# Four two-bank PSUM tiles in place of a four-bank work tile and two fixed pairs, in a delta-rule and mixture-of-experts kernel

## The chip, the core and the metric

The kernel runs on one core of a Trainium2 chip. A core has a matrix engine (TensorE, PE in the profile), three engines for elementwise work (VectorE or DVE, ScalarE or ACT, GpSimd or POOL) and one that issues DMA transfers (SyncE, SP). PSUM is the memory that matrix products go to: eight banks of 512 fp32 numbers in each of 128 partitions in this kernel's use of it. The metric is the device time of the core in microseconds; the figure quoted is the median of several runs.

## The reference

Two computations follow each other. The first is a linear-attention recurrence with a delta rule, for 4 batch entries, 8 heads, 768 tokens and a head dimension of 48:

```
k_n = k / (norm(k) + 1e-6)
for t in range(768):
    y[t]  = q[t] @ state
    v_old = k_n[t] @ state
    state = state + beta[t] * outer(k_n[t], v[t] - v_old)
```

Its output, with the 8 heads side by side, is x (768 tokens of width 384 for each batch entry). The second computation has four attention experts with head dimension 64; two of them are taken for each token:

```
logits = x @ w_gate;  top 2 of 4;  w = softmax over those two
for each expert e:
    q, k, v = x @ wq[e], x @ wk[e], x @ wv[e]
    a  = causal softmax(q k^T / 8)
    ye = a @ v @ wo[e]
    out += w[e] * ye      (where e is among the token's two)
```

Everything is fp32. The kernel computes all four experts for every token and gives the unused ones the weight zero.

## The kernel before, in words

**Blocks.** The work is cut into six units: unit n is batch half n//3 (two batch entries) and token block n%3 (256 tokens). The recurrence is worked in chunks of 64 tokens, c = 0 to 3 in a unit, with 2 batch entries x 8 heads laid over partitions and columns, so that one step of the program is 16 to 64 small matrix products. Within a chunk the recurrence becomes a triangular system, solved once per unit, and the state passes from chunk to chunk.

**The order.** The program has no loop over this work. Each step is a small function, and the string `ORDER` lists steps by name with their arguments, for example `gk.1.0:01` (step gk, unit 1, chunk 0, PSUM banks 0 and 1). The last lines of the kernel walk through the string and call one function after the other under a manual schedule, so this order is the order of the instructions on every engine and in SP's queue. An engine does its instructions one after the other; what one engine needs of another is waited for with semaphores, which the framework puts in from the reads and writes of tiles. A step that writes PSUM carries its place in the string, and a later step that reads it carries the same place.

**PSUM.** Before the change there are three tiles: `PO` (name po in the profile, two banks) for the attention product av and for the dummy products of `fill`; `PA` (pa, two banks) for the state chain; `PR` (pr, four banks) for all else, with `two(k)` giving a pair of banks (any two of the four, "02" is banks 0 and 2) and `one(k)` a single bank.

**The steps**, with the engine that does them. All matrix products go through the helper `mm`, line 175, so PE's instructions have that line in the profile, but for the transposes (L667 and L748).

- Loads, issued by SP: lk (keys and queries of a chunk, two DMAs, 192 KB), lh (one half of it, keys or queries; defined, and not used before), lv (values), lc, ld, lz (constants), lw (weights, split into two fp32r parts by wh on ACT and wl on POOL).
- Preparing a unit: gk (k times k within a chunk) and its readers ek (ACT), or for unit 0 en (DVE) and ed (ACT and DVE); gq (k times q) and its reader eq (DVE). si, so and sn are 32x32 transposes by DVE over a whole unit (L342, L424, L420). pre (DVE) makes the norms. The solve is 15 steps sb on DVE for unit 0 and 32 steps sv on POOL for each other unit (L385, L387).
- Completing the solve: for unit 0 the products zp with their readers ze (ACT or DVE, by i) and preparations zx (the DVE one for chunks is L438); for the others sc1 (ACT), ma, its reader ea (ACT), mc (POOL, L479), mb, its reader eb (ACT).
- The state chain of each chunk: ks, ex (DVE, L507), uu, eu (ACT, L516), st, es (DVE, L530), all on `PA`; vt (POOL, L498) scales the values. The chunk's output: yq, yu into a pair of `PR`, read by eh (ACT, L554) and el (DVE, L558), which split it into two fp32r parts. hx are six small DMAs per half unit that move rows of it to other partitions.
- Projections: pj into one bank, read by ph (ACT, L584) and pl (DVE, L587); pv into two, read by ev (ACT, L600) and eg (DVE, L603); gates (DVE) makes the routing weights.
- Attention: mx (scores for the row maximum) and its reader em (DVE, L651); mp, mr, er (L671) bring the maximum to the layout of the scores; sc (scores) and its reader xp (ACT, exp, L705); av, with the readers oa (ACT, L731) and ob (DVE, L735); nm (DVE, L739 to L742) scales.
- Output: ft (transposes, L748) into one bank, read by fh (ACT, L751) and fl (DVE, L754); fo (times wo) for each 128 tokens into one bank, read by eo (ACT, L765); do (SP, L769) stores 128 tokens.
- `fill` runs a number of dummy products (tile zb) that nothing reads.

Buffers: eight for a chunk's keys and queries, three for its values, two for a unit's system (`TG`, `BB`), three for exp scores (`AT`), two output tiles `OT`.

Of the kernel before, what the change touches and what calls it, by code (L numbers as in the profile page):

```python
# [46 lines left out]
sb.1 en.2:01 sb.2 sb.3 sb.4 sb.5 sv.1.1 sv.1.2 sb.6 sv.1.3 sb.7 sv.1.4 sb.8 sb.9 sv.1.5 sb.10 sv.1.6 sb.11 sb.12
sv.1.7 sb.13 sb.14 sv.1.8 sb.15 sv.1.9 so.0 sv.1.10 sv.1.11 zx.0.0 sn.0 fill.8 zp.0.1:2 sv.1.12 zp.0.0:3 ze.0.0:3
sv.1.13 ze.0.1:2 sv.1.14 zx.1.0 fill.8 zp.0.2:0 zx.0.1 zp.0.3:1 sv.1.15 ze.0.2:0 zp.1.0:3 zp.1.1:2 ze.0.3:1 ze.1.0:3
sv.1.16 ze.1.1:2 fill.2 zp.0.4:0 sv.1.17 zx.1.1 ze.0.4:0 zp.1.2:1 ze.1.2:1 zp.1.3:3 zx.2.2 uu.0.0 ze.1.3:3 gk.2.0:02  # L50
eu.0.0 zp.1.4:1 ek.2.0:02 st.0.0 lv.0.3 zx.2.3 es.0.0 zp.2.1:3 ze.1.4:1 ks.0.1 ze.2.1:3 yu.0.0:02 ex.0.1 gq.0.3:13
eh.0.0:02 eq.0.3:13 sv.1.18 el.0.0:02 fill.6 zp.3.0:1 sv.1.19 zp.3.1:3 ze.3.0:1 zp.2.3:0 ze.3.1:3 zp.2.0:2 vt.0.3
ze.2.3:0 zp.3.3:1 ze.2.0:2 zp.3.2:3 sv.1.20 ze.3.3:1 gq.0.2:02 lw.2 ze.3.2:3 zp.2.2:1 sv.1.21 eq.0.2:02 zp.3.4:3
sv.1.22 ze.2.2:1 lv.0.2 ze.3.4:3 gq.0.1:02 eq.0.1:02 zp.2.4:1 sv.1.23 ze.2.4:1 yq.0.1:03 vo uu.0.1 sv.1.24 lk.2.1 wh.2
eu.0.1 sv.1.25 fill.7 st.0.1 vt.0.2 yu.0.1:03 lv.1.0 es.0.1 gq.1.0:12 eh.0.1:03 sv.1.26 ks.0.2 eq.1.0:12 sv.1.27
ex.0.2 fill.2 yq.0.2:12 sv.1.28 el.0.1:03 lk.2.2 uu.0.2 sv.1.29 eu.0.2 gk.2.1:03 hx.0.0 sv.1.30 sv.1.31 ek.2.1:03
yu.0.2:12 st.0.2 lv.1.1 es.0.2 eh.0.2:12 fill.4 gq.1.1:03 sv.1.32 ks.0.3 eq.1.1:03 ex.0.3 fill.2 yq.0.3:03 el.0.2:12
lk.2.3 uu.0.3 eu.0.3 gk.2.2:12 vt.1.0 sn.1 ek.2.2:12 st.0.3 vt.1.1 yu.0.3:03 lv.1.2 wl.2 eh.0.3:03 fill.4 gq.1.2:12
es.0.3 wl.4 eq.1.2:12 ks.1.0 el.0.3:03 gk.2.3:12 so.1 ek.2.3:12 pj.0.0.0:0 hx.0.1 vt.1.2 si.2 ma.1.0:3 sc1.1.1
pv.0.1:12 mc.1.0 ea.1.0:3 pre.2.0 pre.2.1 ph.0.0.0:0 pre.2.2 pj.0.0.1:3 ev.0.1:12 eg.0.1:12 pre.2.3 sc1.1.0 pre.2.4  # L60
pre.2.5 pj.0.1.0:1 pl.0.0.0:0 ph.0.0.1:3 ex.1.0 pl.0.0.1:3 mx.0.1.1.0.0:02 ph.0.1.0:1 sv.2.1 mb.1.0:3 sv.2.2
em.0.1.1.0.0:02 pl.0.1.0:1 sv.2.3 mx.0.0.0.0.0:02 sv.2.4 eb.1.0:3 ma.1.1:1 em.0.0.0.0.0:02 sv.2.5 mx.0.0.1.0.0:02
ea.1.1:1 mc.1.1 pj.0.1.1:3 em.0.0.1.0.0:02 sv.2.6 sv.2.7 mb.1.1:0 ph.0.1.1:3 sv.2.8 pl.0.1.1:3 mx.0.1.0.1.0:12
eb.1.1:0 sv.2.9 em.0.1.0.1.0:12 sv.2.10 fill.7 mx.0.1.0.0.0:13 mx.0.0.1.1.0:02 em.0.1.0.0.0:13 em.0.0.1.1.0:02 sv.2.11
mx.0.0.0.1.0:13 em.0.0.0.1.0:13 pv.0.0:02 sv.2.12 mp.0.0 sv.2.13 yq.1.0:13 ev.0.0:02 eg.0.0:02 gates.0.0 sv.2.14
uu.1.0 lk.3.0 mx.0.1.1.1.0:02 eu.1.0 sv.2.15 em.0.1.1.1.0:02 fill.3 st.1.0 gates.0.1 mr.0.0:0 lv.1.3 sv.2.16 yu.1.0:13
er.0.0:0 eh.1.0:13 es.1.0 fill.4 gk.3.0:02 sv.2.17 el.1.0:13 ks.1.1 ek.3.0:02 sv.2.18 ex.1.1 yq.1.1:13 gates.0.2
lk.3.1 uu.1.1 vt.1.3 gq.1.3:02 mp.0.1 eu.1.1 eq.1.3:02 st.1.1 sv.2.19 yu.1.1:13 lv.2.0 es.1.1 gq.2.0:02 eh.1.1:13
sv.2.20 ks.1.2 eq.2.0:02 ex.1.2 sv.2.21 fill.2 yq.1.2:02 el.1.1:13 lk.3.2 uu.1.2 sv.2.22 eu.1.2 gk.3.1:13 hx.1.0
ek.3.1:13 st.1.2 vt.2.0 yu.1.2:02 lv.2.1 es.1.2 sv.2.23 ks.1.3 eh.1.2:02 yq.1.3:13 ex.1.3 sv.2.24 lk.3.3 el.1.2:02  # L70
uu.1.3 sv.2.25 eu.1.3 gq.2.1:02 sv.2.26 eq.2.1:02 yu.1.3:13 st.1.3 sv.2.27 eh.1.3:13 gk.3.2:02 lv.2.2 es.1.3 sv.2.28
ek.3.2:02 el.1.3:13 vt.2.1 ks.2.0 ex.2.0 gk.3.3:13 hx.1.1 sv.2.29 sv.2.30 ek.3.3:13 pj.1.0.1:0 sv.2.31 si.3 pv.1.1:12
ph.1.0.1:0 sv.2.32 pl.1.0.1:0 pj.1.1.1:3 ev.1.1:12 pre.3.0 vt.2.2 sn.2 pj.1.1.0:0 ph.1.1.1:3 so.2 ph.1.1.0:0
pl.1.1.1:3 sc1.2.0 pl.1.1.0:0 fill.8 ma.2.1:3 eg.1.1:12 sc1.2.1 pre.3.1 ma.2.0:0 mc.2.1 pre.3.2 pre.3.3 pv.1.0:12
ea.2.1:3 mc.2.0 pre.3.4 pre.3.5 ea.2.0:0 mb.2.1:3 eg.1.0:12 gates.1.0 ev.1.0:12 mb.2.0:0 sv.3.1 gates.1.1 eb.2.1:3
sv.3.2 mr.0.1:1 gates.1.2 sv.3.3 pj.1.0.0:2 sv.3.4 eb.2.0:0 er.0.1:1 sv.3.5 sv.3.6 yq.2.0:13 ph.1.0.0:2 uu.2.0 sv.3.7
lk.4.0 pl.1.0.0:2 eu.2.0 sv.3.8 fill.4 mx.1.1.1.0.0:02 yu.2.0:13 em.1.1.1.0.0:02 sv.3.9 st.2.0 eh.2.0:13 lv.2.3 es.2.0
gq.2.3:02 sv.3.10 el.2.0:13 ks.2.1 sv.3.11 ex.2.1 yq.2.1:13 eq.2.3:02 lk.4.1 uu.2.1 sv.3.12 eu.2.1 mx.1.0.0.0.0:02
em.1.0.0.0.0:02 yu.2.1:13 sv.3.13 st.2.1 eh.2.1:13 gk.4.0:02 lv.3.0 es.2.1 vt.2.3 ek.4.0:02 el.2.1:13 ks.2.2 sv.3.14
ex.2.2 sc.0.1.0.0:13 hx.2.0 sv.3.15 mx.1.0.0.1.0:02 xp.0.1.0.0:13 em.1.0.0.1.0:02 sv.3.16 fill.4 gq.2.2:13 eq.2.2:13  # L80
vt.3.0 gk.4.1:02 ek.4.1:02 yq.2.2:13 sv.3.17 uu.2.2 lk.4.2 sv.3.18 eu.2.2 fill.4 mx.1.0.1.1.0:02 st.2.2
em.1.0.1.1.0:02 sv.3.19 yu.2.2:13 lv.3.1 eh.2.2:13 es.2.2 sv.3.20 fill.3 gk.4.2:02 el.2.2:13 ks.2.3 ek.4.2:02 sv.3.21
ex.2.3 yq.2.3:13 lk.4.3 uu.2.3 lv.3.2 sv.3.22 gq.3.1:02 eu.2.3 eq.3.1:02 yu.2.3:13 vt.3.1 sc.0.0.0.0:02 eh.2.3:13
sv.3.23 el.2.3:13 sv.3.24 xp.0.0.0.0:02 gk.4.3:13 hx.2.1 sv.3.25 ek.4.3:13 fill.3 av.0.0.0.0 vt.3.2 sc.0.1.1.0:02
sv.3.26 oa.0.0.0 si.4 sv.3.27 pv.2.1:13 xp.0.1.1.0:02 sv.3.28 sv.3.29 ob.0.0.0 sv.3.30 sv.3.31 pre.4.0 gq.3.0:02
ev.2.1:13 eg.2.1:13 pre.4.1 sc.0.0.1.0:13 lk.5.0 pre.4.2 pre.4.3 sv.3.32 pre.4.4 xp.0.0.1.0:13 pre.4.5 eq.3.0:02
fill.8 pj.2.0.0:1 so.3 pj.2.1.0:3 ph.2.0.0:1 sv.4.1 pl.2.0.0:1 sc1.3.1 sv.4.2 sv.4.3 sn.3 mx.2.1.1.0.0:02 sv.4.4
av.0.0.1.0 ph.2.1.0:3 sv.4.5 pj.2.0.1:1 oa.0.0.1 sc1.3.0 sv.4.6 pl.2.1.0:3 sv.4.7 em.2.1.1.0.0:02 ma.3.1:3 ph.2.0.1:1
sv.4.8 ob.0.0.1 pl.2.0.1:1 mx.2.0.0.1.0:02 sv.4.9 ea.3.1:3 av.0.1.0.0 em.2.0.0.1.0:02 pj.2.1.1:1 sv.4.10 oa.0.1.0
nm.0.0 sv.4.11 ob.0.1.0 mx.2.0.0.0.0:03 sv.4.12 ph.2.1.1:1 av.0.1.1.0 em.2.0.0.0.0:03 mb.3.1:2 oa.0.1.1 sv.4.13  # L90
pl.2.1.1:1 mx.2.0.1.1.1:03 eb.3.1:2 sv.4.14 ob.0.1.1 ma.3.0:1 em.2.0.1.1.1:03 sv.4.15 mx.2.0.0.0.1:03 ea.3.0:1
ft.0.0:2 em.2.0.0.0.1:03 sv.4.16 mb.3.0:0 fh.0.0:2 nm.0.1 sv.4.17 mx.1.0.1.0.0:13 fl.0.0:2 eb.3.0:0 em.1.0.1.0.0:13
sv.4.18 fill.3 fo.0.0.1:2 mp.1.0 sv.4.19 mx.1.1.1.1.0:01 eo.0.0.1:2 fo.0.0.0:3 em.1.1.1.1.0:01 do.0.0.1 sv.4.20
mr.1.0:2 eo.0.0.0:3 pv.2.0:01 er.1.0:2 sv.4.21 do.0.0.0 sv.4.22 sc.1.0.0.0:23 sv.4.23 ev.2.0:01 eg.2.0:01 gates.2.0
sv.4.24 sc.1.0.0.1:01 xp.1.0.0.0:23 gates.2.1 sv.4.25 gates.2.2 mx.2.1.1.1.1:23 xp.1.0.0.1:01 sv.4.26 av.1.0.0.0
em.2.1.1.1.1:23 sv.4.27 mx.2.1.1.1.0:01 mx.2.0.0.1.1:23 sv.4.28 em.2.1.1.1.0:01 av.1.0.0.1 sv.4.29 mc.3.0 oa.1.0.0
em.2.0.0.1.1:23 fill.3 mx.1.1.0.1.0:01 em.1.1.0.1.0:01 mx.2.1.0.1.1:23 sv.4.30 uu.3.0 sv.4.31 eu.3.0 em.2.1.0.1.1:23
fill.3 gk.5.0:01 st.3.0 ob.1.0.0 ek.5.0:01 yu.3.0:23 lv.3.3 es.3.0 sv.4.32 ks.3.1 eh.3.0:23 yq.3.1:01 ex.3.1 lk.5.1
el.3.0:23 uu.3.1 mc.3.1 so.4 eu.3.1 gq.3.3:23 st.3.1 vt.3.3 yu.3.1:01 lv.4.0 eh.3.1:01 eq.3.3:23 sc1.4.0 el.3.1:01
fill.8 gq.4.0:23 eq.4.0:23 mx.2.0.1.1.0:01 hx.3.0 sc1.4.1 em.2.0.1.1.0:01 fill.3 sc.1.0.1.1:23 vt.4.0 sn.4  # L100
sc.1.0.1.0:01 xp.1.0.1.1:23 xp.1.0.1.0:01 gk.5.1:23 es.3.1 ek.5.1:23 fill.4 mx.1.1.0.0.0:01 ks.3.2 em.1.1.0.0.0:01
# [759 lines left out]
```

## Time and profile before

| | |
|---|---|
| median of 3 runs | 821.58 us (816.61 to 832.48) |
| profiled execution | 828.15 us |
| its span, first to last instruction | 826.4 us |
| mean granted TensorE clock | 0.732 of full |
| busy: PE, DVE, POOL, ACT | 69%, 35%, 27%, 24% of the span |
| DMA traffic | 30.04 MB, mean 36 GB/s |

The profile is of one execution, so its durations add up to its own time, 828.15 us, not to the median. "Busy" counts the time in which an engine has an instruction running; PE's busy time holds the dummy products too. A wait row names the engine and tile that waited, the line and engine whose end released it, and then total time, count and longest. A stage in the stretch view is given by its start and end in us from the span's start. The fp32 products are recorded as two instructions each.

### The profile page before, as it was taken

The numbers are of one execution on the slowest core, as the hardware profiler recorded it, in microseconds if no ns is written. First come the engines' busy times: TensorE is split into PE (matmuls) and PEld (weight loads), VectorE is DVE, ScalarE is ACT, GpSimd is POOL, SyncE is SP. The second block draws the span as 40 slices with busy tenths as digits, with TensorE's granted clock in tenths as the row PEclk, the third lists the DMA queues.
The fourth block names the chain that finished last, engine by engine and source line by source line (L and its number), as shares of the span: only waits on it lengthen the run. The fifth ranks groups of instructions, "written<-read, shape, count | busy, mean of one in ns | idle before, by whom it ended". The sixth has DMA issues, their size and how long they took to land. (4 is left out here: it accounts for less than half of the span.)

```text
span 826.4 us, 26105 instructions
## 1 busy us (share of the span) xinstructions
PE 571.5 (69%) x11987; PEld 480.8 (58%) x11987; DVE 292.4 (35%) x627; ACT 194.4 (24%) x344; POOL 225.5 (27%) x385
## 2 busy tenths in 40 slices
...
GB/s 189 127 0 2 21 61 109 3 1 100 78 2 43 67 68 20 3 20 24 46 69 31 21 2 22 11 3 31 59 2 51 30 10 21 17 4 1 18 7 59
DMA packets 15277, 30.04 MB, mean 36 GB/s; under 512 B 2880, under 2 KB 9024, under 8 KB 15168
## 3 DMA queue, kind: packets, MB, share of 16 engines
...
## 5 line engine op out<-in xcount | busy, mean ns | idle before, releaser
L651 DVE TENSOR_REDUCE mx<-pr 128x2 f32<-128x1024 f32 (+3 forms) x48 | 45.7, 956 | 110.1 <-PE pr L175 80.9
L385 POOL TENSOR_TENSOR bl<-bl,tp 128x30 f32<-128x30 f32 (+9 forms) x150 | 77.9, 519 | 11.7
L387 POOL TENSOR_TENSOR tp<-bl 128x30 f32<-128x30 f32 (+9 forms) x150 | 73.8, 492 | 10.9
L175 PE MATMUL pr<-xh,wqkh 128*128 128x256 f32 x288 | 58.9, 355 | 21.3 <-DVE kl L587 5.2
L705 ACT ACTIVATE at<-pr 128x768 f32<-128x768 f32 (+1 forms) x48 | 43.2, 916 | 118.8 <-PE pr L175 108.9
L498 POOL TENSOR_TENSOR kv<-kv,nt 128x384 f32<-128x384 f32 x24 | 20.4, 848 | 181.0 <-DMA kv<-in_kv_dram 150.7
L175 PEld LDWEIGHTS pr<-xh,wqkh 128*128 128x128 f32 x288 | 50.9, 253 | 26.3 <-DVE kl L587 5.7
L175 PE MATMUL pr<-kq 48*64 48x64 f32 x1536 | 46.7, 277 | 28.1 <-ACT at L705 5.9
L175 PE MATMUL pr<-kh,qh 64*128 64x512 f32 (+3 forms) x128 | 35.7, 557 | 41.5 <-DVE kl L587 8.8
L175 PE MATMUL po<-vs,at 64*64 64x65 f32 x2528 | 60.5, 252 | 2.1 <-issue 1.0
L175 PEld LDWEIGHTS pr<-kq 48*64 48x64 f32 x1536 | 38.9, 182 | 38.3 <-ACT at L705 6.8
L175 PEld LDWEIGHTS po<-vs,at 64*64 64x64 f32 x2528 | 54.4, 164 | 8.9 <-issue 4.4
L175 PE MATMUL pr<-qh,kh 64*128 64x256 f32 x192 | 41.2, 425 | 20.8 <-DVE mx L651 8.1
L175 PEld LDWEIGHTS pr<-kh,qh 64*128 64x128 f32 x128 | 16.4, 253 | 54.5 <-DVE ql L587 8.4
L175 PE MATMUL po<-zb 128*128 128x252 bf16 x211 | 44.3, 362 | 1.6 <-DVE zb L178 1.1
L479 POOL MEMSET tt<- 32x512 f32 x20 | 10.4, 518 | 109.8 <-PE pr L175 109.0
L175 PEld LDWEIGHTS pr<-qh,kh 64*128 64x128 f32 x192 | 23.0, 236 | 27.2 <-DVE mx L651 9.8
L175 PE MATMUL pr<-wvgh,xh 128*128 128x260 f32 x144 | 33.6, 373 | 3.3 <-DVE mx L651 2.0
L175 PE MATMUL pr<-qh,kl 64*128 64x256 f32 x192 | 32.0, 330 | 0.0
L175 PE MATMUL pr<-kq,sb 48*48 48x64 f32 x704 | 19.4, 267 | 18.2 <-ACT tt L320 5.2
L175 PE MATMUL pr<-ql,kh 64*128 64x256 f32 x192 | 31.9, 328 | 0.0
L175 PEld LDWEIGHTS pr<-wvgh,xh 128*128 128x128 f32 x144 | 28.7, 272 | 5.2 <-DVE mx L651 2.5
...
## 6 DMA issues: line engine op xcount, KB each, us to landing
kq<-in_kq_dram SPq DMA_DIRECT2D x48, 192.0 KB, 4.0
...
out_dram<-ot SPq DMA_DIRECT2D x24, 192.0 KB, 2.0
...
```

Of the source, the lines that this page charges most:

```text
L175: T.matmul(o, lhsT=a, rhs=b, start=start, stop=stop, skip_group_check=True)
L385: e.tensor_tensor(X[:, a:b, i + 1:], X[:, a:b, i + 1:], tv, op=OP.add)
L387: e.tensor_tensor(tv, R[:, :, i + 1:].to_broadcast([128, w, m]), X[:, a:b, i:i + 1].to_broadcast([128, w, m]), op=OP.mult)
L479: G.memset(TG[n % 2][r + 32:r + 64, MW * q:MW * q + MW, 0:32], 0.0)
L498: G.tensor_tensor(v, v, nt[n % 2][:, c * NP:c * NP + NP, None].to_broadcast([128, NP, HD]), op=OP.mult)
L651: V.tensor_reduce(d, two(k)[:, :, 0:w], axis=AX.X, op=OP.max)
L705: S.activation(at_of(n, b, y, kp)[:, :, 0:w], two(k)[:, :, 0:w], AF.Exp, scale=0.125)
```

## The change

PSUM becomes four tiles `ps0` to `ps3` of two banks each, `PP` in the code. The place in a step's name is now one digit, the tile: `two(k)` is the whole tile, `one(k)` its first bank. The tiles po and pa go; the state chain (ks, ex, uu, eu, st, es) and the attention product (av, oa, ob) take a tile by name, a new one for each step or chain link. `fill` takes a count and a tile and writes its second bank.

Steps that used one bank and come in pairs take the two banks of one tile: pj for queries and keys of a half unit (`isk` 0 and 1), zp by the parity of i, fo for the two halves of 256 tokens. ma and mb run over all 32 systems of a unit at once, into both banks; sc1, ea, mc and eb now go by halves of the partitions and no longer by halves of the systems, and of ea and eb one half is on ACT and the other on DVE. eo copies both halves of an output at once, from one tile of two banks into one `OT` of twice the size, and do stores 256 tokens with one DMA, so that there are 12 eo and 12 do in place of 24. lh is cut into two DMAs by partitions and is used for unit 0, keys and queries separately; the steps lk go from 24 to 20 and lh from 0 to 8.

The order is a new one. The matmuls of `fill` in it go from 210 to 85, and the one in `init` is removed. The number of steps goes from 1427 to 1368; each unit, chunk and head is still computed with the same products.

```diff
-init lk.1.0 lk.0.3 lz lc.0 lk.1.1 lk.0.0 lk.0.2 lk.0.1 lw.0 lk.1.2 lk.1.3 lc.1 lw.1 ld lv.0.1 lw.3 lv.0.0 lc.2 fill.8
-gk.1.0:01 ek.1.0:01 fill.7 gk.0.3:23 en.3:23 ed.3:23 fill.3 gk.1.1:01 ek.1.1:01 fill.4 gk.0.0:23 en.0:23 ed.0:23
-fill.4 gk.0.2:01 ed.2:01 fill.4 gk.0.1:23 wh.0 en.1:23 ed.1:23 wl.0 si.0 fill.8 gk.1.2:23 lw.6 ek.1.2:23 pre.0.0 wh.1
...
-fo.5.0.1:3 oa.5.1.1 ob.5.1.1 nm.5.1 fo.5.0.0:0 eo.5.0.1:3 do.5.0.1 eo.5.0.0:0 ft.5.1:2 do.5.0.0 fh.5.1:2 fl.5.1:2
-fill.8 fo.5.1.1:1 fo.5.1.0:3 eo.5.1.1:1 do.5.1.1 eo.5.1.0:3 do.5.1.0
+init lz lc.0 lh.0.1.0 lh.0.0.0 lh.0.2.0 lc.1 lh.0.3.0 fill.8:0 gk.0.1:0 lw.0 lc.2 ed.1:0 fill.2:1 gk.0.0:1 ld lk.1.1
+ed.0:1 fill.2:2 gk.0.2:2 lh.0.1.1 ed.2:2 lh.0.3.1 fill.6:3 gk.0.3:3 en.2:2 lh.0.2.1 ed.3:3 wh.0 lv.0.0 cb si.0 wl.0
+lk.1.3 cc lk.1.0 lk.1.2 pre.0.0 zm gk.1.1:2 lw.5 pre.0.1 ek.1.1:2 lv.0.1 zt lh.0.0.1 en.1:0 lw.1 lw.3 pre.0.2 lw.4
+lw.6 pre.0.3 pre.0.4 pre.0.5 vt.0.0 gk.1.3:2 en.0:1 ek.1.3:2 sb.1 sb.2 fill.8:0 gk.1.0:0 sb.3 sb.4 ek.1.0:0 sb.5
+fill.8:1 gk.1.2:1 sb.6 sb.7 ek.1.2:1 sb.8 sb.9 wh.5 sb.10 vt.0.1 si.1 fill.8:2 gq.0.0:2 wl.5 lk.2.0 wh.1 pre.1.0 wl.1
+wh.3 pre.1.1 wh.4 wl.3 pre.1.2 wh.6 wl.4 pre.1.3 wl.6 sb.11 sb.12 sb.13 pre.1.4 sb.14 pre.1.5 sb.15 so.0 sv.1.1 sv.1.2
...
+oa.5.1.1:0 ob.5.1.1:0 nm.5.1 fo.5.0.1:2 eo.5.0:2 ft.5.1:3 do.5.0 fh.5.1:3 fl.5.1:3 fill.8:1 fo.5.1.0:1 fo.5.1.1:1
+eo.5.1:1 do.5.1
...
-    PO = ps.tile([128, 2, 512], F32, name="po")
-    PA = ps.tile([128, 2, 512], F32, name="pa")
-    PR = ps.tile([128, 4, 512], F32, name="pr")
+    PP = [ps.tile([128, 2, 512], F32, name=f"ps{i}") for i in range(4)]
 
     def two(k):
-        a, b = (int(x) for x in k)
-        return PR[:, a:b + 1:b - a]
+        return PP[int(k)]
 
     def one(k):
-        return PR[:, int(k)]
-
-    def fill(k=1):
-        for _ in range(k):
-            mm(PO[:, 1, 260:512], ZB[:, 0:128], ZB[:, 0:252], False)
+        return PP[int(k)][:, 0]
+
+    def fill(n, k):
+        for _ in range(n):
+            mm(two(k)[:, 1, 260:512], ZB[:, 0:128], ZB[:, 0:252], True)
...
-    OT = [cp.tile([128, DM], F32, name=f"ot{i}") for i in range(2)]
+    OT = cp.tile([128, 2, DM], F32, name="ot")
...
     def lh(n, c, i):
-        nc.sync.dma_start(kq_of(n, c)[:, i].rearrange("p a b -> p (a b)"), kq[n, c][:, 512 * i:512 * i + 512])
+        for f in (0, 64):
+            nc.sync.dma_start(kq_of(n, c)[f:f + HD, i].rearrange("p a b -> p (a b)"), kq[n, c][f:f + HD, 512 * i:512 * i + 512])
...
-        mm(PO[:, 1, 260:512], ZB[:, 0:128], ZB[:, 0:252], True)
...
     def zp(c, i, k):
-        P, o = one(k).rearrange("p (a b) -> p a b", b=64), NP * c
+        P, o = two(k)[:, i % 2].rearrange("p (a b) -> p a b", b=64), NP * c
...
-    def ea(n, q, k):
-        W, w = one(k).rearrange("p (a b) -> p a b", b=32), BB[n % 2][:, MW * q:MW * q + MW]
-        for r in (0, 64):
-            S.activation(w[r:r + 32], W[r:r + 32], AF.Copy)
-
-    def mc(n, q):
-        for r in (0, 64):
-            G.memset(TG[n % 2][r + 32:r + 64, MW * q:MW * q + MW, 0:32], 0.0)
...
+    def ea(n, r, k):
+        w = slice(64 * r, 64 * r + 32)
+        if r:
+            V.tensor_copy(BB[n % 2][w], mg(k)[w])
+        else:
+            S.activation(BB[n % 2][w], mg(k)[w], AF.Copy)
+
+    def mc(n, r):
+        G.memset(TG[n % 2][64 * r + 32:64 * r + 64, :, 0:32], 0.0)
...
-    AX_ = PA[:, :, 0:192]
+    ax = lambda k: two(k)[:, :, 0:192]
...
-    def ex(n, c):
+    def ex(n, c, k):
-        V.tensor_tensor(XB.rearrange("p (a b) d -> p a (b d)", a=2), kv_of(n, c)[:, 1].rearrange("p (a b) d -> p a (b d)", a=2), AX_, op=OP.subtract)
+        V.tensor_tensor(XB.rearrange("p (a b) d -> p a (b d)", a=2), kv_of(n, c)[:, 1].rearrange("p (a b) d -> p a (b d)", a=2), ax(k), op=OP.subtract)
...
     def pj(n, hb, isk, k):
-        x, P = XH[(2 * n + hb) % 2], one(k).rearrange("p (y b t) -> p y b t", y=2, b=2)
+        x, P = XH[(2 * n + hb) % 2], two(k)[:, isk].rearrange("p (y b t) -> p y b t", y=2, b=2)
...
-    def av(n, b, y, kp):
+    def av(n, b, y, kp, k):
...
-        O = PO[:, :, 0:260].rearrange("p r (x i d) -> p r x i d", x=2, i=2)
+        O = two(k)[:, :, 0:260].rearrange("p r (x i d) -> p r x i d", x=2, i=2)
...
     def fo(n, b, i, k):
-        R = one(k)[:, 0:DM]
+        R = two(k)[:, i, 0:DM]
...
-    def eo(n, b, i, k):
-        S.activation(OT[i], one(k)[:, 0:DM], AF.Copy)
-
-    def do(n, b, i):
-        t = 256 * (n % 3) + 128 * i
-        nc.sync.dma_start(out[2 * (n // 3) + b, t:t + 128], OT[i])
+    def eo(n, b, k):
+        S.activation(OT, two(k)[:, :, 0:DM], AF.Copy)
+
+    def do(n, b):
+        t = 256 * (n % 3)
+        nc.sync.dma_start(out[2 * (n // 3) + b, t:t + 256].rearrange("(i p) d -> p i d", i=2), OT)
```

ma, mb, eb, sc1, ks, uu, eu, st, es, oa, ob, ph, pl and ze change in the same manner as the functions shown.

297 lines of the change are left out of this document (146 added, 151 removed).

## The prediction
> **What bounds the kernel now.** I read the page's head, then the stretches by stage, then the waits of PE, then one stretch of the timeline, instruction by instruction.
>
> ```profile
> span 826.4 us, 26105 instructions
> PE 571.5 (69%) x11987; PEld 480.8 (58%) x11987; DVE 292.4 (35%) x627; ACT 194.4 (24%) x344; POOL 225.5 (27%) x385
> ...
> 0.00:62.70 62.70, 23.70 (x351) 16.14 (x351) 42.09 (x85) 13.01 (x29) 29.64 (x50) 0.78 0.44 104
> 62.70:142.50 79.80, 56.15 (x1603) 48.87 (x1603) 26.14 (x36) 14.98 (x29) 27.14 (x43) 0.76 0.18 49
> 142.50:826.40 683.90, 491.62 (x10033) 415.81 (x10033) 224.14 (x508) 166.38 (x287) 168.71 (x293) 0.72 0.10 29
> ...
> 62.70:142.50 79.80, 6.71 (x35) 3.40 (x35) 0.00 (x0) 0.00 (x0) 0.76 0.18 49
> 142.50:826.40 683.90, 23.83 (x113) 11.44 (x113) 0.00 (x0) 0.00 (x0) 0.72 0.10 29
> ```
>
> The stretch rows give length, then busy time of PE, its weight loads, DVE, ACT, POOL, then PE's granted clock; the last two rows are the dummy matmuls (`fill`, tile zb) alone. I call the stretches A (loads and the first solve), B (unit 0's products) and C (all else). PE is the busiest engine everywhere but in A, and no other engine passes half of C. Yet PE idles 683.90 - 491.62 = 192.28 us in C, and 23.83 us more are dummies: useful PE time there is 467.79 us, in B 56.15 - 6.71 = 49.44 us. So C is bound by what PE waits for:
>
> ```profile
> PE pr L175 <- DVE mx L651: 29.0, 26, 2.3
> PE pr L175 <- ACT at L705: 22.1, 19, 2.3
> PE pr L175 <- DVE kl L587: 15.4, 10, 2.3
> PE pr L175 <- ACT bl L475: 6.5, 4, 2.6
> PE pa L175 <- issue: 2.2, 4, 1.0
> PE po L175 <- ACT at L705: 0.9, 1, 0.9
> ```
>
> These are waits within C: total, times, longest. They are many, none above 2.6 us, and nearly all belong to writes into `pr`; `pa` and `po` cost 3 us. The releasers are readers of `pr`. The timeline shows that they need not be readers of the same banks:
>
> ```profile
> 448.98 0.44 PE L175 MATMUL pr<-mr,sel 64*128 64x256 bf16 x2
> 449.46 1.72 ACT L705 ACTIVATE at<-pr 128x768 f32<-128x768 f32 x2 [2.22 <-PE pr L175]
> ...
> 451.23 1.65 PE L175 MATMUL pr<-xh,wqkh 128*128 128x256 f32 x6 [1.82 <-ACT at L705]
> ...
> 454.59 0.51 PE L175 MATMUL pr<-xh,wqkl 128*128 128x256 f32 x3
> 454.93 0.51 PE L175 MATMUL pr<-woh,oh 128*128 128x384 f32 x2
> ...
> 455.62 0.51 PE L175 MATMUL pr<-woh,ol 128*128 128x384 f32 x2
> ...
> 456.17 0.60 ACT L584 ACTIVATE qh<-pr 128x512 fp32r<-128x512 f32 x1 [4.99 <-PE pr L175]
> ...
> 456.80 0.69 DVE L587 TENSOR_TENSOR ql<-pr,qh 128x512 fp32r<-128x512 f32 x1 [8.47 <-ACT qh L584]
> ...
> 457.55 0.66 PE L748 MATMUL pr<-cst,on 128*128 128x128 f32 x4 [1.42 <-DVE ql L587]
> ```
>
> The order here is xp on banks 01, xp on 23, pj on bank 0, fo on bank 1, ph and pl on bank 0, ft on bank 2. pj starts at 451.23, when the second xp, which reads only banks 2 and 3, is done (449.46 + 1.72 = 451.18). ph could read bank 0 from 455.10, but starts only after fo, on bank 1, ends at 456.13. ft, on bank 2, waits for pl's read of bank 0 to end at 457.49. So every access to `pr` by one engine waits for all earlier accesses by the others, whatever their banks: the four banks act as one buffer, and PE cannot fill one half while ACT or DVE empties the other.
>
> **The change part by part.**
>
> *Four tiles.* With separate tiles this waiting falls away except within one tile. I counted in both orders how many matmul steps PE runs between the last matmul step on a tile and the next one there, wherever a reader came in between. Before (tiles po, pa, pr): 346 hand-overs, 128 with no step between and 125 with one. After: 359, two with none, seven with one, 70 with two, 280 with three or more. A step of pj takes 455.10 - 451.23 = 3.87 us here, fo 1.20 us, ft 0.66 us; the readers take
>
> ```profile
> L651 DVE TENSOR_REDUCE mx<-pr 128x2 f32<-128x1024 f32 (+3 forms) x48 | 45.7, 956 | 110.1 <-PE pr L175 80.9 <-ACT at L705 10.9 <-PE pr L748 5.2
> ```
>
> about 0.6 to 1.2 us. Three steps cover one reader and a short queue. Priced by hand-over: 192.28 us over the 253 tight ones is 0.76 us each; the nine left keep 7 us, and 70 with two steps, at half, 27 us: 34 us is the floor of C's idle, 192 its ceiling if all waits only change place. Between them I take 90: readers that queue behind DVE's two-microsecond transposes, and chains ks, ex, uu, eu, st, es whose results PE needs itself, are not shown by the count. It lies nearer the floor, as the count does.
>
> *Clock.* Useful PE time depends on the clock, 0.72 in C. It is not one level:
>
> ```profile
> 652.60:676.30 23.70, 18.13 (x158) 15.28 (x159) 5.78 (x10) 3.16 (x6) 0.00 (x0) 0.50 0.11 35
> 789.10:826.40 37.30, 27.88 (x727) 23.96 (x723) 5.54 (x14) 12.48 (x20) 0.00 (x0) 1.00 0.10 34
> ```
>
> At 0.50 PE was busy for 77%, at 1.00 for 75%. Fewer short stops should lift it, but the dummies go from 210 to 85 by the orders, and in C from 113 to the last eight, so little is certain. Bounds: 1.00 gives 467.79 x 0.72 = 337 us, 0.72 leaves 468, 0.60 makes 561. I take 0.78: 432 us. [...]
>
> C is then 432 + 90 + 1 (eight fills at 23.83/113 = 0.21 us) = 523 us, instead of 683.9.
>
> *Loads and first solve (A).* PE's long wait and the solve ahead of it:
>
> ```profile
> PE pr L175 <- DVE vs L438: 32.4, 1, 32.4
> ...
> 0.82 1.79 SPq L254 DMA_DIRECT2D kq<-in_kq_dram  x4
> ...
> 3.60 4.79 SPq L254 DMA_DIRECT2D kq<-in_kq_dram  x8
> ...
> 23.13 1.93 DVE L342 STREAM_TRANSPOSE bl<-vs 128x1024 f32<-128x1024 f32 x1
> ...
> 59.94 2.06 DVE L424 STREAM_TRANSPOSE vs<-bl 128x1024 f32<-128x1024 f32 x1
> ...
> kq<-in_kq_dram SPq DMA_DIRECT2D x16, 192.0 KB, 7.1
> ```
>
> The chain is unit 0's keys, gk, ed, the transpose si.0 at 23.13, the solve, so.0 until 62.00. Before, unit 0's keys are among twelve loads of 192 KB (2.3 MB), issued until 8.39 us and landing 7.1 us after issue in the median; then four rounds of gk, en, ed take turns on `pr` with unit 1's gk. Now lh brings only the key half, eight loads of 96 KB (0.77 MB), first; SP issues these with lz, lc.0 and lc.1 in 11 x 0.45 = 5 us, so the last lands near 12 us, each gk has its own tile, and si.0 starts near 13.5 instead of 23.13. The queries' halves come later and are wanted only by gq. DVE's work from si.0 to so.0 is the same but for one masked copy; so A shrinks by 0 (the loads meet the same traffic) to 11, I take 9.5: 53 us. The order puts unit 1's norm (pre.1) into the middle of the solve, so POOL's solve sv.1 starts later than before, but POOL is busy only 27% and not on the path.
>
> *Unit 0's products (B).* Each zp shared `pr` with its neighbours; now pairs of chunks have a tile each. The useful 49.44 us stay; B keeps 27 dummies (5 us at 6.71/35); the idle of 79.80 - 56.15 = 23.65 us falls to 12, as the chain zp, ze, zp still has nothing beside it in places. B: 66 us, between 60 and 80.
>
> *Joined groups.* ea and eb read both banks at once, half on ACT, half on DVE; eo and do go from 24 to 12; sc1 and mc do all chunks at once.
>
> ```profile
> L475 ACT ACTIVATE bl<-pr 32x512 f32<-32x512 f32 x20 | 11.8, 588 | 36.7 <-PE pr L175 19.1 <-PE pr L667 10.8 <-POOL bl L376 6.6
> L765 ACT ACTIVATE ot<-pr 128x384 f32<-128x384 f32 x24 | 11.6, 491 | 55.2 <-PE pr L175 38.8 <-PE pr L667 8.1 <-PE pr L748 4.2
> ...
> DVE lg L603 <- ACT vs L600: 47.7, 10, 8.7
> ...
> SPq L769 <- ACT ot L765: 296.5, 20, 60.3
> out_dram<-ot SPq DMA_DIRECT2D x24, 192.0 KB, 2.0
> ```
>
> Two engines that only read one tile also take turns (eg behind ev, the third row), so ea's halves run one after the other: about 4 x 0.59 = 2.35 us per unit as before, no gain. A joined eo saves at most one fixed part, a few tenths, off the path. One output tile in place of two makes eo wait until the do before it has landed, 2.0 us for 192 KB, an estimated 2 to 4 us for twice that. Behind a waiting eo stand ACT's other readers; only at the very end are two of them close, where ft, fh, fl and two fo (over 3.5 us) lie between: 0 to 1 us, I take 0.5. do waits on SP ahead of lk, lv and hx; there are half as many, so 0, between -3 and +3 with the new places.
>
> Sum: 53 + 66 + 523 + 0.5 = 642.5 us of span. The profiled execution took 828.15 us for a span of 826.4, so 644.3 in its terms; the median of the runs, 821.58, is 0.8% below it: 639, say 640 us.
>
> **The rivals.**
>
> *Full clock.* [...] In this kernel: C's useful part is 337 us, and with steps that short PE outruns its readers, so idle at 25% as in the row at clock 1.00: 337/0.75 = 449, total 53 + 62 + 449 = 565 us. For it: that row; against: half of C is at 0.50 with the same busy share, and the fills go. 8%.
>
> *The waits move.* Single-bank steps (ft, mr) now hold two banks, and po and pa are gone, so readers queue and idle in C stays near 150 at clock 0.72: 53 + 75 + 468 + 150 = 746 us, to 800 if nothing of the 192 goes. For it: PE still issues in order, and DVE's queue is a third full. Against: three steps at each hand-over. [...] 13%, of which 5% end within 2%.
>
> *Slower.* Without its dummies PE stays at clock 0.50 through C: useful 467.79 x 0.72/0.50 = 674, with 90 idle and B at 49.44 x 0.76/0.50 + 12 = 87: 53 + 87 + 674 + 90 = 904 us. With these, 2% slower (843 us of span) is reached when C's mean clock falls below 467.79 x 0.72/(843 - 53 - 66 - 90) = 0.53. For it: 113 fills of C go; against: the long stretch at 1.00 above with eight fills in 37 us. 4%.
>
> **How the numbers follow.** The forecast's own case has clock 0.72 to 0.88 and idle 60 to 130: C from 383 + 60 = 443 to 468 + 130 = 598, with A and B 113 to 133: 556 to 731 us; 75%. The range 570 to 740 holds most of that and the near part of the second rival, leaving out the full clock, the worst waits and the slower case, 2 in 10. About 2% is what a measurement of this kernel can tell from none. Faster by more: 75 + 8 + 8 = 91%; within 2%: 5%; slower: 4%.
>
> **What would show it.** Four tiles: in C the waits of PE for mx and at readers fall from 51 us to under 20, and PE is busy for over 80%. Clock: C's mean above 0.75 with the dummies gone. A: si.0 (L342) before 16 us and PE's wait of 32.4 us ending near 53. B: unit 0's last product before 115 us. I am wrong if PE's idle in C stays above 130 us, if the clock falls under 0.65, or if one of ACT, DVE or POOL is busy for most of C.

## The result, and the profile after

The changed kernel takes 481.73 us in the median of 4 runs (473.88 to 485.26), the kernel before 825.35 us beside it: a ratio of 0.582 (95% interval 0.565 to 0.599). The direction was forecast, the size was not: 481.73 us lies far below the range of 570 to 740 us. The profile below is of the slowest of the four runs (485.26 us); another profiled run of the same kernel, 482.63 us, has C at 384.0 us with PE idle for 40.0 us and clock 0.96, so nothing below hangs on that choice.

The page's head of the changed kernel (span, then busy time, share and instructions of each engine), and PE's clock by slice:

```profile
span 483.6 us, 25713 instructions
PE 410.1 (85%) x11861; PEld 366.2 (76%) x11861; DVE 296.0 (61%) x637; ACT 176.0 (36%) x292; POOL 225.7 (47%) x375
...
PEclk9575999979789998999899959995999999999999
```

DVE and POOL have the same busy time as before and ACT 18 us less; PE's own fell from 571.5 to 410.1 us, and its clock is near full in most slices. The stages, cut where the prediction cut them (A ends where PE's long wait for the first solve ends, B just before the first projection pj.0.0.0): length, busy time of PE, its weight loads, DVE, ACT, POOL, then granted clock; and in the last two rows the dummies in B and C.

```profile
0.00:45.02 45.02, 18.42 (x338) 13.12 (x338) 33.50 (x83) 12.78 (x29) 15.76 (x25) 0.73 0.56 145
45.02:94.06 49.04, 41.84 (x1582) 38.73 (x1582) 26.25 (x38) 16.52 (x30) 40.89 (x67) 0.97 0.26 71
94.06:483.60 389.54, 349.80 (x9948) 314.31 (x9942) 236.23 (x519) 146.73 (x234) 169.09 (x284) 0.94 0.18 51
...
45.02:94.06 49.04, 3.95 (x27) 2.15 (x27) 0.00 (x0) 0.00 (x0) 0.97 0.26 71
94.06:483.60 389.54, 1.02 (x8) 0.78 (x8) 0.00 (x0) 0.00 (x0) 0.94 0.18 51
```

| | before | forecast | after |
|---|---|---|---|
| A | 62.7 | 53 | 45.0 |
| B | 79.8 | 66 | 49.0 |
| C | 683.9 | 523 | 389.5 |
| useful PE time in C, clock | 467.8, 0.72 | 432, 0.78 | 348.8, 0.94 |
| PE idle in C | 192.3 | 90 | 39.7 |

The waits of PE within C (total, times, longest):

```profile
PE ps L171 <- issue: 22.6, 23, 2.4
PE ps L171 <- DVE bl L468: 1.8, 1, 1.8
PE ps L171 <- DVE mx L648: 1.8, 5, 0.6
...
PE ps L171 <- ACT at L702: 0.6, 2, 0.3
```

The waits for readers of the scores, which were 51 us in this view before, are 2.4 us. Over all rows of this view, the waits with a releaser fell from 184.8 us (181 times) to 12.2 us (21 times). More than half of what is left, 22.6 of 39.7 us, has no releaser; before, such stops were 4.1 us.

### The profile page after: what moved, and what is told of

Same layout as the page of the kernel before. It is cut to its first block, busy times and chain, and to the rows that moved or that the text cites. A ratio compares the mean times of both kernels' runs of the same rounds, so it can differ in the third digit from the quotient of the medians.

```text
span 483.6 us, 25713 instructions
## 1 busy us (share of the span) xinstructions
PE 410.1 (85%) x11861; PEld 366.2 (76%) x11861; DVE 296.0 (61%) x637; ACT 176.0 (36%) x292; POOL 225.7 (47%) x375
## 4 chain that ended last, share of the span: by engine, by line
PE 70%; DVE 13%; issue 8%; ACT 4%; POOL 4%; DMA 1%; SPq 0%; DVEq 0%; ACTq 0%; POOLq 0%
PE ps L171 68%; POOL tp L380 2%; POOL bl L378 2%; DVE mx L648 1%; PE ps L745 1%; DVE bl L395 1%; DVE tn L394 1%; DVE ql L584 1%; DVE kl L584 1%; DVE bl L335 1%; DVE rr L357 1%; DMA kq<-in_kq_dram 1%; ACT tt L421 1%; DVE rr L356 1%; POOL bl L369 1%
## 5 line engine op out<-in xcount | busy, mean ns | idle before, releaser
L702 ACT ACTIVATE at<-ps 128x768 f32<-128x768 f32 (+1 forms) x48 | 43.6, 917 | 32.7 <-PE ps L171 30.8
L171 PE MATMUL ps<-vs,at 64*64 64x65 f32 x2528 | 48.6, 222 | 7.5 <-issue 7.2
L171 PEld LDWEIGHTS ps<-vs,at 64*64 64x64 f32 x2528 | 44.1, 136 | 10.2 <-issue 8.6
L171 PE MATMUL ps<-kq 48*64 48x64 f32 x1536 | 39.6, 245 | 12.9 <-DMA kq<-in_kq_dram 7.1
L648 DVE TENSOR_REDUCE mx<-ps 128x2 f32<-128x1024 f32 (+3 forms) x48 | 44.8, 951 | 8.9 <-PE ps L171 8.8
L171 PEld LDWEIGHTS ps<-kq 48*64 48x64 f32 x1536 | 33.1, 155 | 19.8 <-issue 11.0
L171 PE MATMUL ps<-xh,wqkh 128*128 128x256 f32 x288 | 43.8, 288 | 0.0
L171 PEld LDWEIGHTS ps<-xh,wqkh 128*128 128x128 f32 x288 | 38.0, 191 | 1.1 <-DVE ql L584 0.2
L171 PE MATMUL ps<-qh,kh 64*128 64x256 f32 x192 | 34.2, 353 | 0.4 <-DVE kl L584 0.2
L369 POOL TENSOR_TENSOR bl<-bl,nn 128x1024 f32<-128x1024 f32 x5 | 12.2, 2448 | 42.4 <-DVE nn L368 42.4
L171 PE MATMUL ps<-qh,kl 64*128 64x256 f32 x192 | 27.2, 280 | 0.0
## 6 DMA issues: line engine op xcount, KB each, us to landing
kv<-in_kv_dram SPq DMA_DIRECT2D x24, 384.0 KB, 3.5
out_dram<-ot SPq DMA_DIRECT2D x12, 384.0 KB, 3.5
```

Of the source, the lines that this page charges most:

```text
L171: T.matmul(o, lhsT=a, rhs=b, start=start, stop=stop, skip_group_check=True)
L369: G.tensor_tensor(BL, BL, nn[:, None, :].to_broadcast([128, 32, 32]), op=OP.mult)
L648: V.tensor_reduce(d, two(k)[:, :, 0:w], axis=AX.X, op=OP.max)
L702: S.activation(at_of(n, b, y, kp)[:, :, 0:w], two(k)[:, :, 0:w], AF.Exp, scale=0.125)
```

## The experiments

**The new order, on one tile.** The same kernel, with the four tiles made parts of one:

```diff
-    PP = [ps.tile([128, 2, 512], F32, name=f"ps{i}") for i in range(4)]
+    PW = ps.tile([128, 8, 512], F32, name="ps")
+    PP = [PW[:, 2 * i:2 * i + 2] for i in range(4)]
```

> The changed kernel, its order and all its steps, with the four tiles made one tile of eight banks (ps0 to ps3 are then only parts of it). Theory (tile-wide waits): each reader and each product again wait for all earlier accesses to any bank, so the idle time of PE after the first projection goes from 40 us back to at least 150 us, the clock falls from 0.94 to under 0.80, and the time is 720 to 900 us, because this order puts readers of several groups between the products. Rival (the new order, with its joined groups, is what helps): under 560 us.

Measured: 480.10 us, ratio 0.583 (0.578 to 0.587), clock 0.936 over the whole span (0.924 and 0.938 in the two profiles of the changed kernel): no difference. The run did not test the theory, and the reason is worth more than the run. In the built program each reader's wait names a value of PE's semaphore, and so one product. In the kernel before, 193 of 358 such waits name a product later than the reader's own, on another bank of `pr`: that is the waiting for other banks which the prediction read from the timeline. I call such a wait false. In the changed kernel 19 of 352 are false (the other bank of the same tile), but with the one tile of eight banks none of 370. So in these kernels the framework tells banks apart in the tile of all eight banks, and not in a tile of two or four; why, the runs don't say.

**The same order as before, on four tiles.** Every step and dummy, and the order, as before (less the one dummy product of `init`); each group of steps only gets another place:

```diff
-gk.1.0:01 ek.1.0:01 fill.7 gk.0.3:23 en.3:23 ed.3:23 fill.3 gk.1.1:01 ek.1.1:01 fill.4 gk.0.0:23 en.0:23 ed.0:23
+gk.1.0:3 ek.1.0:3 fill.7:2 gk.0.3:2 en.3:2 ed.3:2 fill.3:1 gk.1.1:1 ek.1.1:1 fill.4:0 gk.0.0:0 en.0:0 ed.0:0
```

> The kernel before, its order, its steps and its 210 dummy products unchanged, but each group of steps (a product, its continuation and its readers) is given the longest free one of four tiles of two banks instead of its fixed banks of pr, pa or po. Theory (tile-wide waits): 500 to 580 us, PE idle in the stage after the first projection 50 to 90 us instead of 192, clock 0.85 to 0.93 instead of 0.72. Rival (the order did it): over 700 us. Between the two, 580 to 700 us: the split needs the new order for part of its gain.

Measured: 540.54 us, ratio 0.655 (0.651 to 0.660). The stages of this kernel, cut at the same points of the work, and its dummies in C:

```profile
0.00:58.83 58.83, 23.20 (x350) 15.74 (x350) 42.21 (x85) 13.12 (x29) 29.65 (x50) 0.77 0.46 111
58.83:108.80 49.97, 44.34 (x1603) 40.16 (x1604) 23.40 (x35) 13.52 (x26) 26.36 (x43) 0.89 0.27 76
108.80:537.10 428.30, 375.60 (x10039) 329.50 (x10033) 229.18 (x510) 168.28 (x289) 170.47 (x294) 0.94 0.17 46
...
108.80:537.10 428.30, 17.49 (x113) 9.23 (x113) 0.00 (x0) 0.00 (x0) 0.94 0.17 46
```

With nothing changed but the places, idle in C falls from 192.3 to 52.7 us, useful time from 467.8 to 358.1, and the clock goes to 0.94. In the built program none of the 395 waits of readers is false. Counted as for the prediction, its 396 hand-overs of a tile have none with no step of PE between, 7 with one, 70 with two and 319 with three or more. The distance comes from taking the tiles in turn; the new order isn't needed for it.

**The old order and the old places, in one tile of eight banks.** The finding of the first run, used on the kernel before:

```diff
-    PO = ps.tile([128, 2, 512], F32, name="po")
-    PA = ps.tile([128, 2, 512], F32, name="pa")
-    PR = ps.tile([128, 4, 512], F32, name="pr")
+    PW = ps.tile([128, 8, 512], F32, name="ps")
+    PO, PA, PR = PW[:, 0:2], PW[:, 2:4], PW[:, 4:8]
```

> The kernel before, its order, banks, steps and dummies unchanged, with po, pa and pr as parts of one tile of eight banks. The merged run of the new order has shown that in a tile of eight banks the framework tells the banks apart: in the built program of before, 193 of the 358 waits of readers for PE name a product later than their own; with the one tile it is 49 of 375, those beside interleaved pairs such as 02. Theory (waits for other banks hold PE up, and its stops hold the clock down): 530 to 620 us, PE idle in the last stage 50 to 110 us, clock 0.87 to 0.94. Rival (more places, not fewer waits, made the four tiles fast): over 700 us, since the places are those of before.

Measured: 605.07 us, ratio 0.730 (0.721 to 0.738). Its stage C and the dummies there:

```profile
116.73:602.00 485.27, 408.69 (x10037) 354.62 (x10033) 227.94 (x509) 167.71 (x289) 169.43 (x293) 0.86 0.14 41
...
116.73:602.00 485.27, 19.29 (x113) 9.61 (x113) 0.00 (x0) 0.00 (x0) 0.86 0.14 41
```

Idle 76.6 us, clock 0.86, just under the range that was expected of it. The places are the old ones to the bank, so the 218 us come from the waits alone: false ones went from 193 to 49. Four tiles by turns (540.54 us) are worth a further 65 us, the 49 false waits included.

**The new order on two tiles of four banks**, where 171 of 268 waits are false:

```diff
-    PP = [ps.tile([128, 2, 512], F32, name=f"ps{i}") for i in range(4)]
+    PW = [ps.tile([128, 4, 512], F32, name=f"ps{i}") for i in range(2)]
+    PP = [PW[i // 2][:, 2 * (i % 2):2 * (i % 2) + 2] for i in range(4)]
```

> The changed kernel, its order and steps, with the eight banks as two tiles of four (ps0 and ps1 parts of one, ps2 and ps3 of the other). In the built program 171 of the 268 waits of readers for PE then name a product later than their own, where the changed kernel has 19 of 352. Theory (those waits are what cost the time): PE idle after the first projection from 40 us to 130 to 220, clock below 0.80, 650 to 850 us: the new order by itself is worth little or nothing. Rival (the order, with its joined groups, carries at least half of the gain): under 600 us.

Measured: 613.47 us, ratio 0.744 (0.739 to 0.749): between the two ranges expected, so neither theory had it.

```profile
118.47:610.10 491.63, 390.10 (x9948) 341.51 (x9942) 242.45 (x519) 146.39 (x234) 168.87 (x284) 0.87 0.14 40
...
118.47:610.10 491.63, 1.02 (x8) 0.78 (x8) 0.00 (x0) 0.00 (x0) 0.87 0.14 40
```

Idle in C is 101.5 us and the clock 0.87, both better than the theory said. Two tiles of four cost this order 132 us against four tiles of two. But the new order, false waits and all, is 210 us better than the old one on its three tiles: not "little or nothing". The two parts overlap: split alone 285 us, order alone 210, both 344. "Order alone" is not quite that, since two tiles of four are not the old tiles either, and 105 of the dummies in C are gone. With two tiles the order's 261 hand-overs have 32 with no step between, 88 with one, 110 with two: less room than with four.

**The stops filled, no wait removed.** The kernel before with `fill.4` ahead of 110 products that follow closely on a reader:

```diff
-mb.1.0:3 sv.2.2
+fill.4 mb.1.0:3 sv.2.2
```

> The kernel before with four more dummy products ahead of 110 of the 205 products in the last stage that follow closely (no or one step of PE between) on a reader of pr; the others are left since po is in use there. No wait is removed. Theory (short stops of PE hold the clock down): the dummies fill the stops, the clock in the last stage rises from 0.72 to over 0.85, useful time of PE there falls from 468 us to under 400, and although the 440 dummies cost 50 to 90 us the whole is no slower than before, 740 to 830 us. Rival (the clock does not hang on these stops): the clock stays below 0.75 and the time grows by at least 40 us, to over 860 us.

Measured: 782.42 us (774.56 to 790.89) beside 825.17 us (821.42 to 836.05); the two ranges don't touch. Stage C and its dummies:

```profile
138.81:772.90 634.09, 480.22 (x10469) 394.65 (x10469) 222.43 (x508) 165.98 (x286) 168.63 (x293) 0.87 0.11 31
...
138.81:772.90 634.09, 86.71 (x549) 46.66 (x549) 0.00 (x0) 0.00 (x0) 0.87 0.11 31
```

86.71 us go to dummies, 63 more than before, and the kernel is still 43 us faster by the medians (30 us between the slowest run with the fills and the fastest without): useful PE time is 480.22 - 86.71 = 393.5 us instead of 467.8, since the clock is 0.87 instead of 0.72. No wait was taken out of the program. So short stops, none above 2.6 us in the view of waits, had held the clock down at 0.72.

**Without any dummies.** The changed kernel less its 85 fills, beside the changed kernel once more:

```diff
-init lz lc.0 lh.0.1.0 lh.0.0.0 lh.0.2.0 lc.1 lh.0.3.0 fill.8:0 gk.0.1:0 lw.0 lc.2 ed.1:0 fill.2:1 gk.0.0:1
+init lz lc.0 lh.0.1.0 lh.0.0.0 lh.0.2.0 lc.1 lh.0.3.0 gk.0.1:0 lw.0 lc.2 ed.1:0 gk.0.0:1
```

> The changed kernel once more, beside the three that follow: 474 to 485 us again.

> The changed kernel without any of its 85 dummy products. Theory (the clock hangs on PE's stops, and after the first projection there are few): clock there 0.92 to 0.96 as with them, the dummies mattered only while PE waited for loads and the first solve, the whole within 2% of the changed kernel. Rival (the dummies hold the clock up): below 0.88 after the first projection and over 500 us.

Measured: 483.13 us with them, ratio 0.584 (0.581 to 0.587); 480.54 us without, 0.581 (0.577 to 0.585); the difference is within the intervals. Stages B and C with the dummies, the dummies of B, then B and C without:

```profile
46.14:96.89 50.75, 43.19 (x1581) 39.97 (x1582) 26.19 (x38) 16.53 (x30) 40.88 (x67) 0.93 0.24 69
96.89:480.90 384.01, 344.02 (x9948) 309.30 (x9942) 236.11 (x519) 146.84 (x234) 169.03 (x284) 0.96 0.18 52
...
46.14:96.89 50.75, 4.36 (x27) 2.27 (x27) 0.00 (x0) 0.00 (x0) 0.93 0.24 69
...
42.20:92.76 50.56, 40.89 (x1554) 38.56 (x1554) 26.74 (x38) 16.52 (x30) 40.88 (x67) 0.97 0.25 69
92.76:475.40 382.64, 344.67 (x9941) 309.94 (x9934) 234.23 (x519) 147.28 (x234) 169.27 (x284) 0.95 0.18 52
```

C keeps a clock of 0.95 with no dummy in the whole kernel; since only 8 of the 85 stood in C, the run says no more of dummies there. In B the useful PE time is 43.19 - 4.36 = 38.8 us with the 27 dummies and 40.9 us without, and the stage is as long (50.75 and 50.56 us): they cost what they bring. At the start they cost: without them si.0 starts at 10.35 us instead of 13.27 beside it.

**Unit 1's solve later.** Two kernels made from the one before, with moves of POOL's steps and of the step that these wait for:

```diff
-sv.1.7 sb.13 sb.14 sv.1.8 sb.15 sv.1.9 so.0
+sb.13 sb.14 sb.15 so.0 sv.1.1 sv.1.2 sv.1.3 sv.1.4 sv.1.5 sv.1.6 sv.1.7 sv.1.8 sv.1.9
```

> The kernel before with one move: the nine steps sv.1.1 to sv.1.9 of unit 1's solve on POOL, which stood among unit 0's solve steps sb on DVE, stand behind so.0. Theory (DVE's products with both inputs in SBUF are slowed while POOL reads SBUF): sb.8 falls from 1.16 us to about 0.6, the 15 steps sb from 19 us to about 10, and so.0 ends near 53 us instead of 62. Rival (sb is as slow by itself, and the change's stage A is shorter for another reason): so.0 still ends at 61 to 62 us. Time of the whole: within 2% of before by either.

Measured: nothing moved. sv.1.1 still starts at 42.27 us, sb.8 takes 1.16 us, so.0 ends at 61.02; 833.91 us in one run. The move left the steps of DVE among themselves, and those of POOL, in the order they had: a place in the order moves a step only past others of its own engine. The second move is of pre.1.5, which POOL's solve waits for:

```diff
-pre.1.3 eq.0.0:23 wl.5 pre.1.4 wh.4 pre.1.5
+pre.1.3 eq.0.0:23 wl.5 pre.1.4 wh.4
...
-sb.15 sv.1.9 so.0
+sb.15 sv.1.9 pre.1.5 so.0
```

> The kernel before with pre.1.5 alone moved to stand just ahead of so.0 on DVE. The earlier move left POOL's start where it was (42 us), since POOL does not wait for DVE's place in the order; pre.1.5 is what POOL's solve of unit 1 waits for, so that now it starts about 10 us later, after the steps sb. Theory (DVE's two-input products are slowed while POOL reads SBUF): sb.8 from 1.16 us to about 0.6, the 15 steps from 19 us to about 10, so.0 ends near 53 us instead of 62. Rival (sb is as slow by itself): so.0 at 61 to 62 us. Whole time within 2% of before by either.

Here the steps sv.1.1 to sv.1.9 were left ahead of pre.1.5, so they work on the system before it is scaled and the kernel solves another system; and they start earlier (34.68 us), not later, than before (43.23 us). POOL is busy with them until 43.62 us and then stands still until 50.91: a cleaner test than the one meant. DVE's and POOL's rows of the timeline there:

```profile
43.11 0.63 DVE L400 TENSOR_TENSOR tn<-bl 128x88 f32<-128x88 f32 x1
43.77 0.25 DVE L401 TENSOR_TENSOR bl<-bl,tn 128x88 f32<-128x88 f32 x1
...
43.06 0.56 POOL L384 TENSOR_TENSOR bl<-bl,tp 128x198 f32<-128x198 f32 x1
50.91 2.38 POOL L375 TENSOR_TENSOR bl<-bl,nn 128x1024 f32<-128x1024 f32 x1 [7.29 <-DVE nn L374]
```

The moment POOL stops, DVE's product falls from 0.63 to 0.25 us. By groups, for the two products of the steps sb, in the kernel before, the changed one and this one:

```profile
L402 DVE TENSOR_TENSOR bl<-bl,tn 128x28 f32<-128x28 f32 (+6 forms) x14 | 9.1, 652 | 0.5
L401 DVE TENSOR_TENSOR tn<-bl 128x28 f32<-128x28 f32 (+6 forms) x14 | 7.0, 499 | 0.4
```
```profile
L395 DVE TENSOR_TENSOR bl<-bl,tn 128x28 f32<-128x28 f32 (+6 forms) x14 | 5.3, 381 | 0.5
L394 DVE TENSOR_TENSOR tn<-bl 128x28 f32<-128x28 f32 (+6 forms) x14 | 4.9, 351 | 0.4
```
```profile
L401 DVE TENSOR_TENSOR bl<-bl,tn 128x28 f32<-128x28 f32 (+6 forms) x14 | 4.2, 302 | 0.5
L400 DVE TENSOR_TENSOR tn<-bl 128x28 f32<-128x28 f32 (+6 forms) x14 | 4.1, 294 | 0.4
```

16.1, 10.2 and 8.3 us for the same 28 products; so.0 ends at 52.77 us instead of 62.00, as the theory had it. The whole took 811.90 us in one run. The changed kernel's own timeline says the same:

```profile
27.47 0.27 DVE L394 TENSOR_TENSOR tn<-bl 128x108 f32<-128x108 f32 x1
27.78 1.24 DVE L395 TENSOR_TENSOR bl<-bl,tn 128x108 f32<-128x108 f32 x1
...
27.62 1.27 POOL L284 TENSOR_TENSOR wol<-at,woh 128x512 fp32r<-128x512 f32 x1 [1.85 <-ACT woh L280]
```

There 24 of the 28 products take 0.28 us or less, and four that run beside POOL's vt or wl take 0.86 to 1.24 us.

**The loads of unit 0 whole.**

```diff
-init lz lc.0 lh.0.1.0 lh.0.0.0 lh.0.2.0 lc.1 lh.0.3.0 fill.8:0
+init lz lc.0 lk.0.1 lk.0.0 lk.0.2 lc.1 lk.0.3 fill.8:0
```

> The changed kernel with unit 0's keys and queries loaded whole (lk), as before the change, at the places of the key halves; the eight DMAs of the query halves are gone. Theory (half the bytes ahead of the first transposes is most of the gain in the first stage): si.0 starts at 16 to 18 us instead of 12.7, PE's wait for the first solve ends 3 to 5 us later, the whole 2 to 6 us slower. Rival (the loads are hidden, the four tiles made si.0 early): si.0 within 1 us of 12.7.

Measured: 485.74 us, ratio 0.587 (0.585 to 0.589), beside 0.584 (0.581 to 0.587) for the changed kernel: the intervals overlap, so the whole doesn't tell. si.0 does:

```profile
15.90 1.94 DVE L333 STREAM_TRANSPOSE bl<-vs 128x1024 f32<-128x1024 f32 x1
```

15.90 us, where it was 12.69 in the changed kernel's profile and 13.27 in its second: the halved loads are worth about 3 us, a little less than the theory had (16 to 18 us).

**Both halves of ea and eb on ACT.**

```diff
-        if r:
-            V.tensor_copy(BB[n % 2][w], mg(k)[w])
-        else:
-            S.activation(BB[n % 2][w], mg(k)[w], AF.Copy)
+        S.activation(BB[n % 2][w], mg(k)[w], AF.Copy)
```

> The changed kernel with both halves of ea and of eb on ACT; in the change one is on DVE, and in the profile DVE's half starts only when ACT's has ended. Theory (two engines that only read one tile take turns, so sharing the work gains nothing): 1.01 us twice on ACT instead of 1.01 + 1.22 us in turn, the whole within 1% of the changed kernel, or up to 2 us faster. Rival (DVE's half relieves ACT): 5 us slower or more.

Measured: 480.97 us, ratio 0.582 (0.579 to 0.584): no difference. In the changed kernel DVE's half waits for ACT's, in these rows of DVE's waits; the built program has this wait, as a semaphore value of ACT's half that DVE's half waits for:

```profile
DVE tt L484 <- ACT tt L486: 8.3, 4, 2.6
...
DVE bl L468 <- ACT bl L470: 6.9, 5, 2.4
```

**The loads of units 2 to 5 left out** (the tokens lk and lv of these units taken from the order):

> The changed kernel without the loads of keys, queries and values of units 2 to 5 (its output is then not the reference's; the work on the engines is the same, on old data). What it tells: of PE's idle time after the first projection, 22.6 us in 23 stops have no releaser in the profile; they lie about 128 products apart or at multiples of it, each within 3 us of a load. Theory (PE's own instructions come by DMA and queue behind the loads): these stops fall below 8 us, and the time falls by 10 to 25 us. Rival (PE's fetching is slow by itself at this pace): still 15 us or more of them, time within 8 us of the changed kernel.

Measured: 476.00 us in one run; PE's waits in C begin with

```profile
PE ps L168 <- issue: 17.4, 22, 1.9
```

The stops stay, at 17.4 us instead of 22.6. That the loads have any part in them isn't shown: the kernel without dummies, with all its loads, has 18.6 us of such stops, and 476.00 us lies within the runs of the changed kernel (473.88 to 485.26). So the theory fails, and of the rival only its figures are confirmed; what the stops are is left open.

## Why the prediction was wrong, point by point

The forecast span was 642.5 us and the measured one 483.6. Of the 159 us between them, 83 are useful PE time in C, 50 idle time in C, 17 stage B and 8 stage A.

**What bounds the kernel** was right, with one limit. Readers and products waited for each other across the banks of `pr`: the built program shows 193 such waits, and taking most of them away in two ways, by four tiles and by one tile of eight banks, takes 285 and 218 us off the time. That "the four banks act as one buffer" is a property of a tile of four, not of any tile.

**The idle time in C** was sized wrongly: 90 us taken, 39.7 measured. The count of hand-overs gave 34 us as the floor, and 39.7 is near it, but partly by luck: the floor prices waits for readers, and of these the view has 12.2 us (and leaves 5 us unlisted), while 22.6 us are stops without a releaser, which no count of hand-overs holds. (The count also ran over the whole order, and the 192 us over C alone; within C it is 216 tight hand-overs before, seven and 65 after, and by the same prices 35 us.) So the step that failed is what was added to the floor: readers queued behind DVE's long transposes and the state chain cost PE next to nothing. None of the rows of waits in C but the first passes 1.8 us.

**The clock in C** was the largest error: 0.78 taken, 0.94 measured, and so 83 us of useful PE time (432 against 348.8). The step that failed was to price clock and idle time apart, and to let the vanishing dummies pull against the clock. Both hang on the same stops: filling stops alone raised the clock from 0.72 to 0.87, and in each run that took waits away the clock rose with it, to between 0.86 and 0.94. The runs in one table, by idle share of C:

| kernel | C | PE idle in C | share | useful | clock |
|---|---|---|---|---|---|
| before | 683.9 | 192.3 | 28% | 467.8 | 0.72 |
| stops filled | 634.1 | 153.9 | 24% | 393.5 | 0.87 |
| new order, two tiles | 491.6 | 101.5 | 21% | 389.1 | 0.87 |
| old places, one tile | 485.3 | 76.6 | 16% | 389.4 | 0.86 |
| old order, four tiles | 428.3 | 52.7 | 12% | 358.1 | 0.94 |
| changed | 389.5 | 39.7 | 10% | 348.8 | 0.94 |

Useful time times clock is 328 to 342 us in every row, so the work is the same within 4% and the clock makes the difference. The clock doesn't follow the idle share alone: 24%, 21% and 16% all go with 0.86 or 0.87. What else about the stops counts, their length or their spacing, no run varies by itself. The floor of idle with the useful time at the measured 0.94, 337/0.94 + 34 = 392 us, would have met C, with the luck named above.

The prediction gave a full clock 8%, and tied it to a busy share of 75% taken from a row of before at clock 1.00; that share was the old waits' doing, and PE is now busy for 90% of C. That the change would bring the full clock was the author's estimate: the kernels with four tiles ran C at 0.94 to 0.96.

**Stage A** was forecast at 53 and is 45.0. si.0 starts at 12.69 us (13.5 forecast), for reasons that the runs divide: the four tiles alone bring it to 19.14, and the halved loads are worth 3 us of the rest; what gives the other 3 isn't shown. Less than 1 us of the miss is there. The other 7 us are the step that said "DVE's work from si.0 to so.0 is the same" and that POOL's later solve is "not on the path". It isn't, but it slowed the path: from si.0 to the end of so.0 it was 38.9 us before and is 31.6 now, and 16.1 - 10.2 = 5.9 us of the difference are the 28 products above. The rows of the run with pre.1.5 late show it one product at a time: 0.63 us with POOL busy, 0.25 without, for the same shape. Through what POOL slows DVE, no run shows. The forecast looked only at whether POOL's solve was waited for, and not at what it does to DVE beside it.

**Stage B** was forecast at 66 and is 49.0. Its idle time is 49.04 - 41.84 = 7.2 us (12 forecast), and its useful time 41.84 - 3.95 (27 dummies) = 37.9 us, where the forecast left 49.44, at the old clock of 0.76; it is 0.97 now. That is the clock's error again.

**Joined groups and outputs** were rightly held to bring nothing by their sharing of engines: 1.01 + 1.22 = 2.23 us in turn for ea, 2.35 forecast. A joined eo takes 0.81 us where two took 2 x 0.49, and a store of 384 KB lands 3.5 us after issue in the median, within the 2 to 4 us estimated. That C of the changed kernel is 38.8 us below the old order on four tiles has other sources: dummies 17.49 - 1.02 = 16.5 us, idle 13.0, useful time 9.3. Which steps of the order give the last two isn't shown.

**The rivals.** Waits that only move did not come: 39.7 us of idle. The clock in C did not fall for want of dummies: 0.94 with eight, 0.95 with none. Full clock was nearest in kind, and gave 565 us because it took the idle share of before.

**The checks named ahead**: waits for mx and at 2.4 us (under 20), PE busy 349.80/389.54 = 90% of C (over 80%), clock 0.94 (over 0.75), si.0 at 12.69 (before 16), all as said; PE's first wait ends at 45.0, not near 53. The check on unit 0's last product (before 115 us) was a weak one: it ended at 117.1 before and ends at 75.8 now.
